# Transposing DMA transfers in place of TensorE turns, from the fifth group on, in a gated linear attention with a maxout feed-forward

## The chip, the cores and the metric

The kernel runs on one core of a Trainium2 chip. The metric is the device time of one execution in microseconds; smaller is better. The engines are TensorE (PE, with its weight loads PEld), VectorE (DVE), ScalarE (ACT), GpSimd (POOL) and SyncE (SP). SyncE computes nothing here: it issues the DMA transfers of the inputs and of the output. GpSimd issues those of the four weight matrices.

## The reference, cut to what matters

Four batches, eight heads, 768 steps, 48 channels a head. Each head carries a 48 x 48 state that decays channel by channel; the output of all heads is a row of 384 for each token, and the rows go through a maxout feed-forward.

```python
for t in range(S):                      # q, k, v, alpha: (4, 8, 768, 48), float32
    state = alpha[:, :, t, :, None] * state + np.einsum('bhd,bhe->bhde', k[:, :, t], v[:, :, t])
    y[:, :, t] = np.einsum('bhd,bhde->bhe', q[:, :, t], state)
...
h = np.maximum(np.maximum(x @ w1, x @ w2), x @ w3)     # x: (3072, 384), w: (384, 768)
return (h @ w_out).astype(np.float32)                  # w_out: (768, 384)
```

## The kernel before, in words

**Tiles.** A group `n` (0 to 11) is 256 tokens of one batch, all heads; `c, b = divmod(n, 4)`. A unit `u` is half the heads of a group, `u = 2n` or `2n + 1` (0 to 23). A partition of the input tiles holds two neighbouring tokens (`r` = 0, 1) of a block of 128 tokens; 64 partitions are one block (`i` = 0, 1).

**Steps of a group.** `load` (L262, SyncE) brings alpha, q, k and v, 384 KB each, into five buffers each. `decay` (L317) takes logarithms of alpha and group totals (`hp`). `prep(u)` (L380) makes running sums of the logarithms on TensorE (`Lp`, L389), exponentials of both signs (`ep`, `en`, L398), weights q and k with them (`qk`, L403, on GpSimd or VectorE), and turns them so that channels lie on partitions: `tp` (L421) is 16 TensorE transposes of 64 x 128 into two PSUM banks, and `qkT` (L429) one VectorE copy of 128 x 1024 out of them. Scores `A` (L441) are 16 small products of the turned k and q, and `LA` (L449) masks them. `state(n)` (L456) sums the new state (`pp`, L472) and carries it on (`Z`, L373). `output(n)` (L496) adds the part of the old state (`yi`, L509) and of the scores (`ya`, L531); for each of the two blocks, `xb` (L543) scales the result into 128 x 384, `xp` (L551) turns it with three TensorE products by a permutation matrix `order`, which also puts the tokens back in their order, and `xT` (L556) copies it out of PSUM.

**Feed-forward.** `ffn(n)` (L560) uses `w2 - w1` and `w3 - w1` (`wcat`; the differences `d`, L281): 36 products, `gp` (L575), in six steps of six per group: three column pairs `j`, each for gate `g` = 0 and 1. `h0` and `h1` (L584, L591) take the maxima. `op` (L603, L606) gives the output of one block, `ob` copies it, and `out` (L618, SyncE) stores it. `past` (L307) is `w1 @ w_out`.

**Order.** Every piece above is a step of a `Plan`, numbered as the loops create it (before: 0 to 810). A string, `ORDER`, lists all steps in the sequence in which they are issued: `24P3` is step 24 on TensorE with PSUM bank 3, and the letters P, V, A, G, S stand for TensorE, VectorE, ScalarE, GpSimd and SyncE. It was made ahead of time; nothing is chosen on the chip. Every engine works through its own tokens in this sequence and waits where an operand isn't ready. So on SyncE a transfer that waits holds all behind it. The four weight transfers (`weights`, L272) are tokens of GpSimd's sequence: w1, w2 and w3 are tokens 6, 7 and 10 of GpSimd's.

Of the kernel before, what the change touches and what calls it, by code (L numbers as in the profile page):

```python
# [23 lines left out]


ORDER = """
6S 0S 3S 1S 2S 52S 5S 7S 8V 9A 4S 10A 11G 17P0 54S 18V 13A 53S 19A 14P1 98S 28P2 12A 20A 55S 29V
15A 22V 100S 30A 31A 21V 99S 56V 101S 24P3 16G 143S 58A 32V 145S 57A 33V 74P5 144S 59P6 25V 62P7
35P0 146S 23A 63V 205S 26P2 64A 36V 272S 65A 34A 206S 75V 37P0 67G 27V 207S 60A 40P47 77A 274S 76A
61G 339S 66V 208S 42V 78G 69P2 38V 273S 39G 79V 41V 73G 81P5 68A 102G 82V 70V 83P0 80G 104A 44P4  # L30
85G 84V 86P56 45P2 87V 71P0 88V 46A 119P3 72V 103A 47P5 90P2 49A 120V 91P4 122A 193P0 92V 95A 105P1
121A 89V 108P4 93P2 48A 43V 96P3 50P6 123V 51A 94A 124V 109V 126P5 111A 97A 195P7 189V 106A 187V
196A 262P2 127V 321P3 194A 188V 128P5 110A 113V 254P1 112G 129V 258P7 255A 130G 329P0 115P4 192V
330A 197P1 107G 116V 114A 125G 331P6 198A 190V 117P4 325P0 322A 118V 147G 148A 256P1 191V 149A
131P34 263A 257V 153P5 259A 264P2 154V 133V 326A 132V 164P1 260P7 156A 265V 327P0 165V 261V 167A
135P3 323P2 166A 332V 155A 136P7 324V 169G 201P1 140V 158G 150P6 199P5 202A 137A 157V 151A 168V
160P2 328V 171P6 203P1 159A 170G 172V 200A 161V 173P6 204A 175P05 209G 174V 162P2 333P1 211A 163V
276G 277A 210A 218P6 269P7 334A 152G 219V 539S 278A 176V 275S 134V 221A 340S 177V 220A 141P2 229P3
138P1 341S 285P4 222G 230V 179P0 139A 266P6 142V 406S 231A 286V 342S 232A 223V 288A 234G 279P1
180P2 270A 267V 287A 212P3 178V 392P7 181A 233V 213A 296P6 225P4 280A 215G 184A 297V 236P2 290G  # L40
394P1 226V 299A 298A 237V 301G 182P0 393A 388P4 183V 344A 185P5 343G 238P2 395V 224A 227P6 336P0
186A 228V 289G 235A 389A 214G 239V 217G 390P1 337A 216G 345A 292P5 338S 300G 240P74 473S 293V 363P0
352P2 396P3 408S 353V 241V 474S 354A 463P5 391V 397A 268S 242G 398P6 335S 291A 282G 243V 409S 461P7
464A 281G 364V 302G 407S 399V 366A 459P3 284G 271S 365A 244V 476S 245P1 355A 246P5 460V 307P60 671S
357G 247P 462V 605S 294P2 251A 465P4 283G 295V 248A 356G 252P7 411A 455P5 253A 308V 368G 457P1 456A
466V 249P2 359P6 410G 458V 250A 303P3 346P5 529P2 304V 310G 412A 525P1 360V 309G 347A 530A 367G
305P3 311V 369A 361P5 521P7 306V 526A 349G 350G 358A 312P2 523P0 351G 522A 362V 543G 313P1 413P3
419P4 430P7 314P 414A 431V 370P5 420V 433A 467P3 524V 315A 435G 371V 318A 421A 477G 372P0 422A
374P25 545A 470P6 436G 479A 375V 478A 348G 373V 376G 432A 379P4 434G 480P2 471A 403P7 468A 424V
377V 486P0 319P1 423G 404A 531P6 487V 378V 488A 405S 380P3 527P7 481A 532V 608S 320A 541S 489A 381P  # L50
609G 528V 544A 475S 426P1 437P5 382A 540S 415G 316P0 427V 503G 400P7 317A 438V 416G 385V 383P4
552P1 401V 386P2 384A 591P0 483V 387A 402S 553V 484G 428P5 672S 592A 439P3 675G 497P7 555A 655P2
440V 554A 425G 593P0 611A 485G 498V 589P1 500A 418V 429V 491G 546P3 499A 653P4 587P7 417G 654A 594V
441P56 547A 676A 490V 563P4 533P3 442V 588V 443G 444G 656V 661P0 534A 501G 564V 447P5 535S 663P7
590V 662A 606S 492G 677A 446P2 445V 657P3 674S 565A 502G 664V 542S 566A 493P0 448P 658V 472S 482G
556G 504P6 607S 494V 508P4 624A 469S 659P3 452A 449V 610A 618P0 505V 595P1 450P5 453P2 596V 597P6
451A 454A 509V 536P7 660V 511G 549G 619V 568G 598V 621A 506P1 495P4 620A 678P3 551G 537A 725P6 496V
569G 679A 538S 684P0 612P7 719P3 557G 673S 685V 507V 665P4 567G 550V 686A 629P5 695P1 548V 599P2
510V 613A 720A 681V 623V 666A 615V 683V 723P7 622G 696V 630V 698A 602P3 724V 631A 614G 558G 687A
726V 635A 688G 721P4 697A 600V 603A 512P7 700G 601S 513P0 722V 632A 625P1 667S 514P 604S 626V 699G  # L60
574P6 515A 559P3 570P1 518A 727P5 634G 571V 701A 519P7 575V 729P0 616G 728A 560V 577G 516P1 668P2
633G 517V 730V 520V 627P5 669A 572P3 689V 561P0 737P7 670S 617V 573V 731P2 738A 562V 741P7 732A
578P3 576V 745P4 742A 628V 690A 579P0 636P1 580P 637V 640P7 581A 691P5 584V 638P1 746A 582P3 692V
747P0 583A 641V 644P4 743P5 639V 642G 739P6 643G 680V 585P3 645P7 740V 702P1 586A 646P 682V 706P3
703V 647A 734P6 650A 748V 707V 744V 704P1 709G 693P3 759P7 708G 735V 694V 755P0 757P5 705V 711P6
752P3 710P4 761P1 753A 756A 754S 648P2 712P 760A 733S 651P3 649A 749P0 762V 652A 716V 713V 777P7
750A 763P2 751S 736S 717P1 714P3 781P6 718A 779P4 782V 765P0 715V 783P1 778V 799P6 764V 801P3 766V
800A 773P7 784V 775P2 758V 793P0 780V 797P6 774V 795P1 791P5 767P4 792V 802V 770P7 776V 768A 796V
769S 794V 785P5 798V 771V 803P3 786V 772S 787S 807P4 804P 808P 805V 788P2 809A 806S 810S 789A 790S
"""  # L70


# [41 lines left out]
def kernel(  # L114
# [12 lines left out]
    nc = tc.nc  # L127

    B, H, S, D = q.shape
# [3 lines left out]
    P = 128  # L133
    HALF = P // 2
# [6 lines left out]
    UB = 2  # L141
# [13 lines left out]
    both = np.eye(2)  # L155
# [30 lines left out]
    NL, NQ, NT_, HH = 5, 6, 4, H // 2  # L186
    ld = {x: homes(NL, [P, H, 2, D], FP32, x + "n") for x in "aqkv"}
# [49 lines left out]

    live = {}
    LEAD, SLOPE = 5.5, 1.9
    WAFTER = {2: (0,), 4: (1,), 7: (2,), 11: (3,)}  # L240

    def copy(eng, out, in_):
        (nc.scalar.copy if eng == "ACT" else nc.vector.tensor_copy)(out=out, in_=in_)  # L243
# [136 lines left out]
    def prep(u):  # L380
# [1 line left out]
        hs = slice(hh * HH, (hh + 1) * HH)  # L382
        la, ep, en = las[n % 3], eps[u % 3], ens[u % 3]
        qk, v16 = qks[u % NQ], v16s[u % NQ]
        Lk, tk, Ak = ("Lp", u), ("tp", u), ("A", u)

        def cums(eng):
# [11 lines left out]
                          out=t, in_=live[Lk], func=AFT.Exp, scale=sign),  # L399
                      reads=[Lk, (Lk, 0)], writes=[(x, u % 3)])  # L400
        for w, x, e in ((0, "q", ep), (1, "k", en)):
            plan.step("qk", "POOL DVE", u,
                      lambda eng, w=w, x=x, e=e: on[eng].tensor_mul(  # L403
                          qk[:, w, :, :, :D].rearrange("p r h d -> p h r d"),
                          ld[x][n % NL][:, hs], e),
                      reads=[(x, n % NL, hh), ("ep" if w == 0 else "en", u % 3)],
                      writes=[("qk", u % NQ, w)])
        plan.step("v", "POOL ACT", u,
# [4 lines left out]
        def trans(eng):  # L413
            live[tk] = banks2(tk, FP16)[:, :, :4 * P]
            for w in range(2):
                for j in range(2):
                    for r in range(2):
# [4 lines left out]
                                                qk[rows, w, r, 2 * j:2 * j + 2, :],  # L422
                                                ident[rows, rows])

        plan.step("tp", "PE", u, trans, banks=[tk],
                  reads=[("qk", u % NQ, 0), ("qk", u % NQ, 1)],
                  writes=[tk])
        plan.step("qkT", "DVE", u,
                  lambda eng: nc.vector.tensor_copy(  # L429
                      out=qkT.rearrange("p i w j t -> p i (w j t)"), in_=live[tk]),  # L430
                  reads=[tk], writes=[("qkT", u % NT_)])

        def scores(eng):
            live[Ak] = banks2(Ak, FP32)
# [21 lines left out]
    def state(n):  # L456
# [6 lines left out]
        def sums(eng):  # L463
            for k in keys:
                live[k] = bank(k, [P, NP, 2 * D], FP32)
            for hh in range(2):
                qk, v16 = qks[us[hh] % NQ], v16s[us[hh] % NQ]
                for j in range(2):
                    for r in range(2):
                        for i in range(n_i):  # L470
                            rows = slice(i * HALF, (i + 1) * HALF)
                            nc.tensor.matmul(live[keys[i]][:, 2 * hh + j, :],  # L472
                                             qk[rows, 1, r, 2 * j:2 * j + 2, :],
                                             v16[rows, 2 * j:2 * j + 2, r, :],
                                             start=(r == 0), stop=(r == 1))

# [19 lines left out]
    def output(n):  # L496
# [43 lines left out]
        for i in range(UB):  # L540
# [4 lines left out]
                          eng, xb, live[yk].rearrange("p a b -> p (a b)"), ysc),  # L545
                      reads=[yk], writes=[("xb", m % 3)])

            def turn(eng, xb=xb, xk=xk):
                live[xk] = bank(xk, [P, NFT, P], FP32)
                for ft in range(NFT):  # L550
                    nc.tensor.matmul(live[xk][:, ft, :], xb[:, ft * P:(ft + 1) * P], order,  # L551
                                     start=True, stop=True)

            plan.step("xp", "PE", rank, turn, banks=[xk], reads=[("xb", m % 3)], writes=[xk])
            to = xTs[n][:, :, i * P:(i + 1) * P]
            plan.step("xT", "DVE ACT", rank, lambda eng, to=to, xk=xk: copy(eng, to, live[xk]),  # L556
                      reads=[xk], writes=[("xT", n, i)])


    def ffn(n):  # L560
# [32 lines left out]
        for i in range(UB):  # L593
# [4 lines left out]
            for lo, hi in parts:  # L598
                def shrink(eng, i=i, ok=ok, lo=lo, hi=hi):
# [5 lines left out]
                    for kt in range(lo, hi):  # L605
# [8 lines left out]
                          + ([("xT", n, i)] + [("past", kt) for kt in range(NFT)]) * (lo == 0))  # L614
            plan.step("ob", "ACT DVE", r, lambda eng, m=m, ok=ok: copy(eng, obs[m % 4], live[ok]),
                      reads=[ok], writes=[("ob", m % 4)])
            plan.step("out", "SP", -2.0,
                      lambda eng, i=i, m=m: nc.sync.dma_start(  # L618
                          out[b * S + (2 * c + i) * P:b * S + (2 * c + i + 1) * P, :], obs[m % 4]),
                      reads=[("ob", m % 4)])  # L620

    load(0, 0, HH, "aqk")
# [52 lines left out]
```

## Time and profile before

| | us |
|---|---|
| median of 2 timed runs (151.75 to 153.57) | 152.66 |
| the profiled execution | 153.0 |
| its span, first to last instruction | 151.2 |
| TensorE busy | 133.5 |
| VectorE busy | 120.7 |
| ScalarE busy | 82.3 |
| GpSimd busy | 69.3 |

How to read the profile: it is one execution, times in microseconds from the start of the span. "xN" is a number of instructions. The 40 slices give the busy share of each fortieth of the span in tenths. A group names the line, engine, operation and tiles, then busy time and mean duration. "SPq" is SyncE issuing a transfer; the time from there to the landing of the data is listed apart. A line with three numbers and slashes gives the shortest, the median and the longest duration in ns. TensorE's products overlap, so the sum of their durations is longer than the time that they take. The granted TensorE clock is 0.998 of full speed.

### The profile page before, as it was taken

How to read it: one execution, taken by the hardware profiler on the slowest of the kernel's cores; microseconds unless marked ns; L12 is line 12 of the kernel's file. 1: busy time of each engine (PE TensorE's matmuls, PEld its weight loads, DVE VectorE, ACT ScalarE, POOL GpSimd, SP SyncE). 2: the span in 40 equal slices, each digit the busy share in tenths (PEclk: the TensorE clock that was granted, in tenths of full speed). 3: DMA queues.
4: the chain of work that ended last, by engine and by line, in shares of the span. 5: the costliest groups of instructions: out<-in, count | busy, mean ns of one | idle time of the engine just before them, and what ended most of it. 6: DMA issues, size and time to landing. Idle time of an engine off the chain costs nothing.

```text
span 151.2 us, 5265 instructions
## 1 busy us (share of the span) xinstructions
PE 133.5 (88%) x2220; PEld 102.4 (68%) x2220; DVE 120.7 (80%) x210; ACT 82.3 (54%) x185; POOL 69.3 (46%) x106
## 2 busy tenths in 40 slices
PE   0145498999999999999999999998999999999991
PEld 0133276677766778888677878766868877888660
DVE  3188988769999999999698998899899992395920
ACT  3467246829576996777967756536627305210111
POOL 8114920080390697798992865688800220000000
PEclk9999999999999999999999999999999999999999
DMA  5999999999999999999529929960410002300124
GB/s 127 273 261 261 266 213 211 240 249 221 279 260 262 262 252 261 282 310 270 114 59 259 290 60 259 255 191 0 160 56 0 4 4 81 127 4 0 52 104 156
DMA packets 55880, 26.45 MB, mean 175 GB/s; under 512 B 50737, under 2 KB 55857, under 8 KB 55857
## 3 DMA queue, kind: packets, MB, share of 16 engines
q1 hardware_dynamic: 53440, 23.60, 63.5%
q0 software_dynamic: 1984, 2.36, 9.0%
q8 instruction: 17, 0.28, 0.8%
q10 hardware_dynamic: 432, 0.17, 0.5%
q14 instruction: 7, 0.05, 0.1%
HBM read 23.76 MB, written 4.72 MB: 188 GB/s over the span
## 4 chain that ended last, share of the span: by engine, by line
PE 74%; DMA 11%; SPq 5%; DVE 3%; issue 3%; ACT 2%; POOL 1%; ACTq 0%; DVEq 0%; POOLq 0%
PE psum L575 31%; PE psum L606 14%; PE psum L603 7%; DMA wcat<-in_moe_w_dram 7%; SPq L262 5%; PE psum L441 4%; DMA qn<-in_q_dram 4%; PE psum L421 4%; PE psum L531 3%; PE psum L472 3%; PE psum L551 2%; PE psum L307 2%; PE psum L509 2%; PE psum L389 1%; DVE Z L373 1%
## 5 line engine op out<-in xcount | busy, mean ns | idle before, releaser
L575 PE MATMUL psum<-xT,wcat 128*128 128x256 f16 x432 | 55.3, 277 | 0.3 <-DVE wcat L281 0.3
L575 PEld LDWEIGHTS <-wcat 128*128 128x128 f16 x432 | 40.7, 99 | 6.6 <-DVE wcat L281 0.5
L449 DVE TENSOR_TENSOR LA<-psum,d 128x1024 f16<-128x1024 f32 x24 | 28.8, 1219 | 3.8 <-PE psum L441 2.6
L606 PE MATMUL psum<-wo,hT 128*128 128x384 f16 x144 | 27.3, 326 | 0.0
L591 DVE TENSOR_TENSOR hT<-psum,hT 128x512 f16<-128x512 f32 x36 | 23.8, 681 | 3.2 <-PE psum L531 2.8
L403 POOL TENSOR_TENSOR qk<-qn,ep 128x384 f16<-128x384 f32 x16 | 16.7, 1052 | 14.5 <-ACT ep L398 14.0
L243 ACT COPY ob<-psum 128x384 f32<-128x384 f32 x17 | 8.1, 484 | 24.7 <-PE psum L606 24.7
L403 POOL TENSOR_TENSOR qk<-kn,en 128x384 f16<-128x384 f32 x15 | 15.0, 1001 | 13.0 <-ACT en L398 8.5
L606 PEld LDWEIGHTS <-hT 128*128 128x128 f16 x144 | 14.1, 98 | 9.3
L584 ACT ACTIVATE hT<-psum 128x512 f16<-128x512 f32 x25 | 14.6, 600 | 8.1 <-PE psum L575 7.9
L429 DVE COPY qkT<-psum 128x1024 f16<-128x1024 f16 x24 | 16.0, 684 | 1.4 <-PE psum L421 1.1
L603 PE MATMUL psum<-past,xT 128*128 128x384 f16 x72 | 15.7, 327 | 0.0
L421 PE MATMUL psum<-d,qk 64*128 64x64 f16 x384 | 10.6, 200 | 5.2 <-DVE qk L403 4.0
L398 ACT ACTIVATE en<-psum 128x384 f32<-128x384 f32 x24 | 11.8, 496 | 5.3 <-DVE psum L393 4.1
L398 ACT ACTIVATE ep<-psum 128x384 f32<-128x384 f32 x24 | 11.7, 492 | 4.6 <-POOL qk L403 2.9
L373 POOL TENSOR_TENSOR Z<-U,G 48x192 f16<-48x192 f32 x12 | 6.0, 504 | 16.3 <-DVE U L486 15.8
L421 PEld LDWEIGHTS <-qk 64*128 64x128 f16 x384 | 8.1, 100 | 8.0 <-DVE qk L403 5.3
L243 ACT CAST xT<-psum 128x384 f16<-128x384 f32 x19 | 8.8, 483 | 6.0 <-PE psum L551 5.7
L324 POOL TENSOR_TENSOR aa<-an 128x384 f32<-128x384 f32 (+1 forms) x11 | 10.7, 972 | 2.6 <-DMA an<-in_alpha_dram 2.5
L247 ACT ACTIVATE xb<-psum,c 128x384 f16<-128x384 f32 x17 | 9.4, 580 | 4.2 <-PE psum L531 4.1
L586 DVE TENSOR_SCALAR hT<-psum 128x512 f16<-128x512 f32 x11 | 7.5, 686 | 4.4 <-PE psum L575 4.3
L247 ACT ACTIVATE v<-vn,c 128x384 f16<-128x384 f32 x14 | 8.6, 617 | 4.3 <-DMA vn<-in_v_dram 3.9
(54 smaller groups left out, 193.8 us busy)
## 6 DMA issues: line engine op xcount, KB each, us to landing
out_dram<-ob SPq DMA_DIRECT2D x24, 192.0 KB, 2.0
an<-in_alpha_dram SPq DMA_DIRECT2D x11, 384.0 KB, 6.1
kn<-in_k_dram SPq DMA_DIRECT2D x11, 384.0 KB, 5.9
qn<-in_q_dram SPq DMA_DIRECT2D x11, 384.0 KB, 6.5
vn<-in_v_dram SPq DMA_DIRECT2D x11, 384.0 KB, 6.1
wcat<-in_moe_w_dram POOLq DMA_DIRECT2D x2, 576.0 KB, 11.3
w1s<-in_moe_w_dram POOLq DMA_DIRECT2D x1, 576.0 KB, 8.0
wo<-in_moe_w_out_dram POOLq DMA_DIRECT2D x1, 576.0 KB, 7.6
```

What stands on the lines that cost most here:

```text
L243: (nc.scalar.copy if eng == "ACT" else nc.vector.tensor_copy)(out=out, in_=in_)
L247: nc.scalar.activation(out=out, in_=in_, func=AFT.Copy, scale=factor)
L398: lambda eng, t=t, sign=sign: nc.scalar.activation(out=t, in_=live[Lk], func=AFT.Exp, scale=sign),
L403: lambda eng, w=w, x=x, e=e: on[eng].tensor_mul(qk[:, w, :, :, :D].rearrange("p r h d -> p h r d"), ld[x][n % NL][:, hs], e),
L421: nc.tensor.transpose(live[tk][:, i, at:at + HALF], qk[rows, w, r, 2 * j:2 * j + 2, :], ident[rows, rows])
L429: lambda eng: nc.vector.tensor_copy(out=qkT.rearrange("p i w j t -> p i (w j t)"), in_=live[tk]),
L449: lambda eng: nc.vector.tensor_mul(LA.rearrange("p a j r t -> p (a j) (r t)"), live[Ak].rearrange("p a (j t) -> p (a j) t", j=2), maskA.un ...
L575: nc.tensor.matmul(live[gk][:, jj, :], wcat[:, kt, g, c0:c0 + P], xT[:, kt, :], start=(kt == 0), stop=(kt == NFT - 1))
L584: nc.scalar.activation(out=h, in_=live[gk], func=AFT.Relu)
L591: lambda eng, h=h, gk=gk: nc.vector.tensor_max(h, live[gk], h),
L603: nc.tensor.matmul(live[ok], xT[:, kt, i * P:(i + 1) * P], past[:, kt, :], start=(kt == 0), stop=False)
L606: nc.tensor.matmul(live[ok], hT[:, kt, i * P:(i + 1) * P], wo16[:, kt, :], start=False, stop=(kt == NJ - 1))
```

## The change

Two constants, `DQ = DX = 4`, mark the first group that is treated in the new way.

- For units of groups 4 to 11 (16 units), `tp` and `qkT` are gone. A step `dq` on SyncE issues two transposing DMA transfers instead, one per block, each from 64 partitions x 1024 columns of `qk` straight into `qkT`.
- For these units the columns of `qk` are laid out so that a head pair's two tokens lie side by side, and each weighting is done by two instructions, one per pair of heads (`qk2`); the sums `pp` read the same columns in the new place.
- For the 16 blocks of these groups, `xp` and `xT` are gone. A step `dx` on SyncE issues one transposing transfer from `xb` (128 x 384) into `xT`. The tokens stay in the turned order, even ones first, and the store of the output is issued as two transfers of 64 rows each, every second row of the output.
- `ORDER` is new from the first token on, for 779 steps. SyncE now has 52 loads, 16 `dq`, 16 `dx` and 24 `out` tokens. GpSimd's w1, w2, w3 are tokens 7, 10 and 17 of its own sequence; ahead of w3 stand, among others, weightings of units 4, 5 and 6.

```diff
+    DQ, DX = 4, 4
...
+        qkx = qk.rearrange("p w r h d -> p (w r h d)").rearrange(
+            "p (w j r a d) -> p w j r a d", w=2, j=2, r=2, a=2)
+        cross = n >= DQ
...
+            def weigh(eng, w=w, x=x, e=e):
+                src = ld[x][n % NL][:, hs]
+                if not cross:
+                    on[eng].tensor_mul(qk[:, w, :, :, :D].rearrange("p r h d -> p h r d"), src, e)
+                else:
+                    for j in range(2):
+                        part = slice(2 * j, 2 * j + 2)
+                        on[eng].tensor_mul(
+                            qkx[:, w, j, :, :, :D].rearrange("p r a d -> p a r d"),
+                            src[:, part], e[:, part])
...
+            def swap(eng):
+                for i in range(UB):
+                    rows = slice(i * HALF, (i + 1) * HALF)
+                    nc.sync.dma_start_transpose(
+                        qkT[:, i].rearrange("p w j (r s) -> p (w j r) s", r=2),
+                        qk[rows].rearrange("p w r h d -> p (w r h d)"))
+
+            plan.step("dq", "SP", u, swap, reads=both, writes=[("qkT", u % NT_)])
...
+                            if n >= DQ:
+                                key = qk[rows, 1].rearrange("p r h d -> p (r h d)")[
+                                    :, (2 * j + r) * P:(2 * j + r + 1) * P]
...
+            else:
+                plan.step("dx", "SP", rank,
+                          lambda eng, to=to, xb=xb: nc.sync.dma_start_transpose(to, xb),
+                          reads=[("xb", m % 3)], writes=[("xT", n, i)])
...
+            rows = out[b * S + (2 * c + i) * P:b * S + (2 * c + i + 1) * P, :]
+            if n >= DX:
+                rows = rows.rearrange("(s r) d -> r s d", r=2)
+
+            def store(eng, rows=rows, m=m):
+                if len(rows.shape) == 2:
+                    nc.sync.dma_start(rows, obs[m % 4])
+                else:
+                    for r in range(2):
+                        nc.sync.dma_start(rows[r], obs[m % 4][r * HALF:(r + 1) * HALF, :])
```

## The prediction

> **What bounds the kernel now.** I read the page's busy line and its slices first, then the chain, then TensorE's instructions in order of time, then the SyncE queue and the landing times of its transfers.
>
> ```profile
> span 151.2 us, 5265 instructions
> PE 133.5 (88%) x2220; PEld 102.4 (68%) x2220; DVE 120.7 (80%) x210; ACT 82.3 (54%) x185; POOL 69.3 (46%) x106
> ...
> PE   0145498999999999999999999998999999999991
> ...
> DMA  5999999999999999999529929960410002300124
> ```
>
> From about 28 us to 148 us TensorE has no empty slice, and the DMA engines are full up to about 75 us, then free in places. The waits of TensorE in 28 to 148 us come to 0.8 us. So the kernel is a start, a closed stream of products, and a tail of 3.3 us. The chain in order of time shows what ends the start: the second weight matrix.
>
> ```profile
> 16.76 10.67 DMA wcat<-in_moe_w_dram
> 27.53 0.57 DVE wcat L281
> 28.14 2.74 PE psum L575 x12
> ```
>
> What one step is worth to the stream is the distance to the next start, not its duration:
>
> ```profile
> 52.25 0.25 PE L389 MATMUL psum<-la,c 128*128 128x192 f16 x1
> 52.43 0.64 PE L421 MATMUL psum<-d,qk 64*128 64x64 f16 x32
> 53.00 0.83 PE L575 MATMUL psum<-xT,wcat 128*128 128x256 f16 x6
> 53.67 0.33 PE L551 MATMUL psum<-d,xb 128*128 128x128 f16 x3
> 53.83 0.82 PE L575 MATMUL psum<-xT,wcat 128*128 128x256 f16 x6
> ```
>
> Two tp steps (32 transposes) take 0.57 us, so one takes 0.29; an xp step takes 0.16 to 0.18 (0.18 used); a gp step 0.66. In the same way A is 0.30, ya 0.52, yi 0.20, pp 0.45, Lp 0.20, hp 0.12, an op 1.46. Adding these along the order of before, from the first gp on, gives 119.1 us; the profile has 28.1 to 147.9, 119.8. The units are good to 0.7 us.
>
> The SyncE queue and its landings:
>
> ```profile
> L262 SPq DMA_DIRECT2D kn<-in_k_dram x13: 418/1067/8338, 0.7 to 97.8; - x13
> L262 SPq DMA_DIRECT2D an<-in_alpha_dram x13: 496/1294/3515, 1.2 to 68.8; - x13
> L262 SPq DMA_DIRECT2D qn<-in_q_dram x13: 385/1416/3292, 2.3 to 89.8; - x13
> L262 SPq DMA_DIRECT2D vn<-in_v_dram x13: 380/783/2107, 6.0 to 91.0; - x13
> ```
>
> ```profile
> L618 SPq DMA_DIRECT2D out_dram<-ob x24: 332/359/3108, 57.5 to 148.4; - x24
> ```
>
> A load holds SyncE for 0.4 us when the queue is free and for 1.4 when it is full; a store for 0.36 us. A store lands 4.1 us after its issue (median) while loads run (66 to 100 us) and 1.9 us after it later. This queue has slack now; it is where the change puts everything.
>
> **The change, part by part.** I numbered the steps of both orders as the loops make them, and put every SyncE token of the new order against the TensorE work listed ahead of it ("stream time": first gp at 28.1).
>
> *Removed, TensorE.* 16 tp at 0.29 and 16 xp at 0.18: 7.5 us. The new order also has 1.9 us more work ahead of the first gp (10.05 against 8.17 us). From the first gp on 109.7 us are left: 28.1 + 109.7 + 0.7 + 3.3 gives a span of 141.8 us if nothing waits. This is the gain to be had: 9.4 us.
>
> *Removed, VectorE and ScalarE.* 16 qkT copies at 684 ns (10.9 us of VectorE) and 16 xT copies at 483 to 551 ns. TensorE hardly waits for either in the stream (1.1 us for qkT by its weight loads, inside the 7.5), so no further gain: 0.
>
> *Split products.* Each weighting becomes two of 192 columns. On GpSimd two cost 2 x 504 ns (the row of Z at 192) against 1,000, on VectorE 2 x 357 (aa at 192) against 550: 9 of them, 1.5 us, under the 10.9 us that VectorE is freed of. 0; without that cover at most 1.5.
>
> *Second store from group 4 on.* 16 more issues of 0.36 us; one is at the end: +0.4 on the span.
>
> *A start listed anew.* GpSimd starts the weights. Before, the second and third follow the first at 16.8 and 19.1 us. In the new order the third (gate 1) stands behind qk of group 3, which reads q of group 3, the load that before was issued from 27.7 to 31.0 us behind three weights. With two weights ahead of it, each worth (31.0 - 15.8)/3 = 5.1 us of the queue, its issue ends near 25.9; 6.6 us to landing, 1.0 for the product: the third weight starts near 33.5, lands 7.6 to 8.0 us later, and after 0.6 us of differences the first gate-1 product can start at 42.1 us. Stream time has it at 28.1 + (16.58 - 10.05) = 34.6, the listed work up to it. I take +7.5 us. Bounds: 0 if loads and weights share otherwise; +11.2 if it lands in 11.3 us like wcat before.
>
> *Added: 48 transposing DMAs on SyncE* (32 of 64 x 1024, 16 of 128 x 384). No row shows one. Low end: a store, 0.36 us of SyncE, landing 1.6 us after its issue ends. High end: the load in a full queue, 1.44 us. I take 1.14, the mean of the loads' four medians, since a transpose is cut into small pieces as the loads are (384 bytes there) and not as the stores (1,536). For the landing I take the store amid loads, 4.1 us from the start, 2.96 after the issue, and 0.76 after it once the loads are over; a load is taken at 0.45, a store at 0.36.
>
> What is queued behind them: SyncE waits in order, so a dq whose qk isn't ready holds loads and stores too, and a load lost there delays the next qk. The cover is the TensorE work listed between the transfer and its reader: 4.0 to 8.2 us for dq, 1.8 to 7.9 for dx. Two examples. The dq of unit 12 has dq 11, dq 10, a load and both dx of group 4 in front, free to start at 52.7: 52.7 + 4 x 1.14 + 0.45 + 2 x 1.14 + 2 x 1.14 = 62.2, lands 65.2, and A of unit 12 stands at 61.8: 3.4 late (1.2 of it already due to dq 11). The second dx of group 8 stands only 1.8 us ahead of its product and needs 1.14 + 2.96: 2.3 late. Down the whole queue in this way: dq 11 1.2, dq 12 2.2, dx 5 0.9, dq 15 0.9, dx 6 0.5, dx 8 2.3, dq 20 0.4, dx 9 1.6, dx 10 and a small one 0.5: 10.5 us of new waits. At the low end it is 0.2, with 1.44, loads at 1.40 and stores at 0.80 it is 24 to 37.
>
> [...] The rows bound a transposing DMA only by its neighbours. [...]
>
> *Sum.* 141.8 + 7.5 + 10.5 + 0.4 = 160.2 us of span. The profiled execution took 153.0 us at a span of 151.2 (+1.8); the median of the timed runs, 152.66, is 0.3 under it. So 160.2 + 1.8 - 0.3 = 161.7, rounded to 162.
>
> **Rivals.**
> - *The transfers are hidden* (on the other side: not slower). Place: dq and dx on SyncE. At the store's price the leads hold and 0.2 us of waits remain: 141.8 + 7.5 + 0.2 + 0.4 + 1.5 = 151.4. It decides where the waits stay under 4.5 us (155.7 or less): issues under 0.6 us at the landings taken, or under 1.05 us if they land 1.6 us after the issue. For it: leads of mostly 4 us and more, free DMA slices after 75 us. Against: stores amid loads land in 4.1 us.
> - *The weights come in time as well*: no 7.5, 143.9. For it: the order of before met its weights to 0.8 us. Against: the load of q 3 above.
> - *Weights in time, queue as forecast*: 154.2.
> - *SyncE and the DMA rings become the bound.* The transposes add 5.8 MB to 26.5 MB, queue behind loads, and every issue costs a full queue's price: 24 to 37 us of waits, 175 to 188. For it: loads held SyncE 1.4 us each up to 56 us. Against: slices of DMA at 0 to 4 tenths after 105 us. [...]
>
> **How the numbers follow.** Forecast 0.48, its own range 155 to 169 (issues 0.95 to 1.3 us, weights +4 to +11). Hidden 0.15, hidden with weights in time 0.12, weights in time alone 0.07, rings the bound 0.18. Two per cent of 152.66, about what a measurement of this kernel can tell from no change, puts the limits at 149.6 and 155.7: faster 0.12; within, 0.15 + 0.07 = 0.22; slower, 0.48 + 0.18 = 0.66. The range 148 to 181 leaves out the fastest case (0.12) and the upper part of the slowest (0.08), 0.2 together.
>
> **What would show it.** In the profile after: DMA_TRANSPOSE issues on SyncE with a mean of 1 us or more, landing 3 us or more later; TensorE idle before the scores (A) and before gate products, released by DMA, some 8 to 12 us; the first gate-1 product later than 38 us; VectorE busy near 110 us. The prediction is wrong if these waits are under 2 us, if the issue takes under 0.5 us or over 2 us, or if the gate-1 weights land before 36 us.

## The result, and the profile after

The changed kernel takes 184.96 us (median of 2 runs, 183.75 to 186.17) against 152.66: slower, ratio 1.2116, 95% interval 1.1656 to 1.2576. The forecast of 162 had the direction and not the size. The profiled execution took 186.17 us, its span is 184.4.

First the page of the changed kernel: busy line, slices, and the shares of the chain.

```profile
span 184.4 us, 4767 instructions
PE 140.7 (76%) x1916; PEld 100.7 (55%) x1916; DVE 123.3 (67%) x223; ACT 72.8 (39%) x162; POOL 65.4 (35%) x116
PE   0245549967999989299798699978769869499960
PEclk9999999999999999969999699999987987969996
DMA  6999999999949978499996999699868965516154
...
PE 36%; SPq 23%; DMA 18%; DVE 14%; ACT 3%; issue 3%; POOL 1%; DVEq 0%; POOLq 0%
```

Before, TensorE had no empty slice from 28 us on; now it has holes all along. It runs 304 instructions fewer and is busy 7.2 us longer: PEclk, before at 9 in every slice, drops to 6 to 8 in several. In the chain SyncE's issues (SPq) went from 5% to 23%.

SyncE's instructions by line (three numbers: shortest, median and longest, in ns), with the landings counted from the start of the issue:

```profile
L447 SPq DMA_TRANSPOSE qkT<-qk x32: 1200/1262/2533, 51.5 to 153.2; - x32
DMA to landing us min/median/max: 2.6/3.3/5.6
...
L587 SPq DMA_TRANSPOSE xT<-xb x16: 1179/1206/3180, 70.5 to 164.5; - x16
...
L657 SPq DMA_DIRECT2D out_dram<-ob x32: 466/593/2153, 129.8 to 181.2; - x32
```

A transposing issue never takes less than 1.18 us here. The mean is 1.41, since some are held longer, up to 3.18; what held those is not shown. From 51.4 to 165.8 us, 114.4 us, SyncE is held for 101.1: 44.8 by the 32 transfers of q and k, 22.8 by the 16 of the outputs, 17.0 by 24 loads (0.71 each), 16.4 by 22 stores (0.75). (The texts of the experiments say 1.45, 0.77 and 103.5: they count the short gaps between neighbouring issues as held.) That queue is nearly full, and works in order: in the rows of it below, no issue starts before the one ahead of it has ended.

What TensorE waits for, in order of time, and SyncE at one of these places:

```profile
77.16 0.24 PE L461 MATMUL psum<-qkT 48*64 48x128 f16 x2 [2.40 <-DMA qkT<-qk]
91.20 2.12 PE L606 MATMUL psum<-xT,wcat 128*128 128x256 f16 x18 [1.17 <-DMA xT<-xb]
102.91 1.46 PE L606 MATMUL psum<-xT,wcat 128*128 128x256 f16 x6 [1.78 <-DMA xT<-xb]
160.61 1.20 PE L606 MATMUL psum<-xT,wcat 128*128 128x256 f16 x6 [2.35 <-DMA xT<-xb]
```

```profile
95.23 1.81 SPq L447 DMA_TRANSPOSE qkT<-qk  x1
97.14 1.21 SPq L587 DMA_TRANSPOSE xT<-xb  x1
98.39 0.57 SPq L262 DMA_DIRECT2D kn<-in_k_dram  x1
99.02 1.25 SPq L587 DMA_TRANSPOSE xT<-xb  x1
100.31 0.58 SPq L262 DMA_DIRECT2D qn<-in_q_dram  x1
```

The xT issued at 99.02 comes behind two transposes and a load without a gap, and its reader starts at 102.91, 3.9 us later. The loads behind it are late in turn. By the waits of the whole kernel, GpSimd stands 14.9 us for alpha (2.5 before), 13.1 for k (4.6 before) and 12.7 for v.

### The profile page after: what moved, and what is told of

The parts are those of the page before. It is cut to its first block, busy times and chain, and to the rows that moved or that the text cites. A ratio compares the mean times of both kernels' runs of the same rounds, so it can differ in the third digit from the quotient of the medians.

```text
span 184.4 us, 4767 instructions
## 1 busy us (share of the span) xinstructions
PE 140.7 (76%) x1916; PEld 100.7 (55%) x1916; DVE 123.3 (67%) x223; ACT 72.8 (39%) x162; POOL 65.4 (35%) x116
## 2 busy tenths in 40 slices
DMA packets 80197, 32.19 MB, mean 175 GB/s; under 512 B 75056, under 2 KB 80176, under 8 KB 80176
## 4 chain that ended last, share of the span: by engine, by line
PE 36%; SPq 23%; DMA 18%; DVE 14%; ACT 3%; issue 3%; POOL 1%; DVEq 0%; POOLq 0%
PE psum L606 18%; SPq L262 11%; DMA xT<-xb 6%; SPq L447 6%; PE psum L637 6%; DMA qn<-in_q_dram 4%; DMA out_dram<-ob 3%; SPq L587 3%; DMA vn<-in_v_dram 3%; DVE LA L469 3%; PE psum L634 3%; DVE qk L408 2%; SPq L657 2%; DVE qk L412 2%; PE psum L496 2%
## 5 line engine op out<-in xcount | busy, mean ns | idle before, releaser
L606 PE MATMUL psum<-xT,wcat 128*128 128x256 f16 x432 | 59.3, 289 | 9.4 <-DMA xT<-xb 6.1
L412 POOL TENSOR_TENSOR qk<-kn,en 128x192 f16<-128x192 f32 x24 | 13.8, 600 | 14.5 <-DMA kn<-in_k_dram 13.1
L412 POOL TENSOR_TENSOR qk<-qn,ep 128x192 f16<-128x192 f32 x22 | 12.8, 603 | 15.1 <-ACT ep L401 10.0
L634 PE MATMUL psum<-past,xT 128*128 128x384 f16 x72 | 16.4, 337 | 0.4 <-DVE U L510 0.4
L461 PE MATMUL psum<-qkT 48*64 48x128 f16 x384 | 11.4, 240 | 4.3 <-DMA qkT<-qk 3.7
L401 ACT ACTIVATE en<-psum 128x384 f32<-128x384 f32 x24 | 11.2, 488 | 8.0 <-DVE psum L396 6.6
L324 POOL TENSOR_TENSOR aa<-an 128x384 f32<-128x384 f32 (+1 forms) x7 | 6.6, 942 | 20.2 <-DMA an<-in_alpha_dram 14.9
L432 PE MATMUL psum<-d,qk 64*128 64x64 f16 x128 | 5.4, 225 | 10.0 <-DVE qk L408 8.8
L392 PE MATMUL psum<-la,c 128*128 128x192 f16 x24 | 6.2, 282 | 8.7 <-ACT la L334 7.9
L461 PEld LDWEIGHTS <-qkT 48*64 48x64 f16 x384 | 7.4, 116 | 8.7 <-DMA qkT<-qk 4.3
L617 DVE TENSOR_SCALAR hT<-psum 128x512 f16<-128x512 f32 x14 | 9.5, 684 | 1.7 <-PE psum L606 1.7
L432 PEld LDWEIGHTS <-qk 64*128 64x128 f16 x128 | 3.7, 114 | 12.2 <-DVE qk L408 9.6
```

Of the source, the lines that this page charges most:

```text
L401: lambda eng, t=t, sign=sign: nc.scalar.activation(out=t, in_=live[Lk], func=AFT.Exp, scale=sign),
L412: on[eng].tensor_mul(qkx[:, w, j, :, :, :D].rearrange("p r a d -> p a r d"), src[:, part], e[:, part])
L461: nc.tensor.matmul(live[Ak][i * HALF:(i + 1) * HALF, p, at:at + P], qkT[rows, i, 1, j, r * HALF:(r + 1) * HALF], qkT[rows, i, 0, j, :], st ...
L606: nc.tensor.matmul(live[gk][:, jj, :], wcat[:, kt, g, c0:c0 + P], xT[:, kt, :], start=(kt == 0), stop=(kt == NFT - 1))
L634: nc.tensor.matmul(live[ok], xT[:, kt, i * P:(i + 1) * P], past[:, kt, :], start=(kt == 0), stop=False)
```

## Experiments

All but 16 and 17 are single runs, and differences under 2 us between them are not read; the kernel before took 152.9 to 153.9 us beside them. "Q" is the theory that SyncE's in-order queue is overfull; the others are named in the texts.

**1. The new order with the turns on TensorE.** Each tp with its copy stands where dq stood, each xp where dx stood.

```diff
-    DQ, DX = 4, 4
+    DQ, DX = 12, 12
```

> The changed kernel with its new order, but every turn back on TensorE: each dq is a tp and a qkT copy at the same place of the order (or at the next place where two PSUM banks are free), each dx an xp and an xT copy on ScalarE, stores undivided. Theory Q (SyncE's queue: a transposing DMA holds SyncE about 1.45 us, in order, so 48 of them and the loads and stores behind them set the pace): the queue falls free, the late start of about 11 us and 7.5 us of turns on TensorE stay: 155 to 165 us. Theory O (the new order itself is what loses the time): 175 us or more. Theory R (the DMA engines and the landing of data are what is short): as Q, 155 to 165, since the transposes' bytes are gone too.

189.3 us. Useless as a test: TensorE, itself in order, now meets each tp directly ahead of the copy out of PSUM and waits for it (11.0 us of its waits end with a copy `qkT`, 4.3 with an `xT`). Run 11 mends that.

**2. Plain copies of the same bytes**, without transposing, at the same places.

```diff
-                    nc.sync.dma_start_transpose(
-                        qkT[:, i].rearrange("p w j (r s) -> p (w j r) s", r=2),
-                        qk[rows].rearrange("p w r h d -> p (w r h d)"))
+                    nc.sync.dma_start(
+                        qkT[:, i].rearrange("p w j t -> p (w j t)"),
+                        qk[:, i].rearrange("p r h d -> p (r h d)"))
```

> The changed kernel with each transposing transfer replaced by a plain SBUF-to-SBUF copy of the same number of bytes into the same tile (the turn itself is left out, so the output isn't the reference's). Same order, same waits, same count of issues. Theory Q: an issue costs about 0.6 us instead of 1.45, 48 x 0.85 = 41 us of SyncE's 103.5 us are gone, and what remains is the late start and short landings: 153 to 162 us. Theory R: bytes and queue places are the same, so 175 to 185. Theory O: 175 or more.

165.85 us. The issue of the copy, by line:

```profile
L446 SPq DMA_DIRECT2D qkT<-qk x32: 465/551/1776, 51.2 to 135.2; - x32
```

0.55 us (median) in place of 1.26. 32.20 MB moved against 32.19, landing 3.0 us after the start against 3.3 (qkT) and 3.6 (xT). So the bytes aren't the price: the transposing is. The time lies between the ranges of Q and R, and run 3 shows why it is above Q's. The copies also make fewer packets (67,142 against 80,197), so this run does not tell SyncE's hold from work inside the DMA engines.

**3. The transfers left out**, the rest as in the change. The two transfers of `dq` go in the same way, and `ffn` reads a tile of an earlier group, `xTs[n % 4]`.

```diff
-                          lambda eng, to=to, xb=xb: nc.sync.dma_start_transpose(to, xb),
+                          lambda eng: None,
```

> The changed kernel with the 48 transposing transfers left out altogether: scores and feed-forward of groups 4 to 11 read what groups 0 to 3 left in the tiles. It shows the floor of the new order with its late start. Theory Q and theory R: 150 to 156 us (141.8 us of listed work and tail, and about 11 us of late start). Theory O: 165 or more.

166.34 us (span 164.6): as with plain copies. Those were wholly hidden. But I had expected 150 to 156: without any transfer and without any turn in groups 4 to 11, the new order still ends 12 us behind the kernel before (153.89 beside it). Runs 4, 9, 10 and 13 to 15 look for these.

**4. The weights early**: w2 and w3 (73G, 85G) directly behind w1 (39G).

```diff
-109V 150P3 39G 82V 122A 148A 41V ... 110A 73G 46A
+109V 150P3 39G 73G 85G 82V 122A 148A 41V ... 110A 46A
```

> The changed kernel with one edit of its order: the transfers of w2 and w3 stand right behind that of w1 on GpSimd, as in the kernel before, instead of 3 and 10 tokens later. Theory Q: the products start some 5 to 10 us earlier, but SyncE's stretch from the first dq to the last dx (114 us, 103.5 of them held) stays as long and only begins somewhat earlier: 176 to 183 us. If the late start alone is the cause: 170 us or less.

183.68 us. The third weight now starts at 20.4 us, 13.1 earlier, and the first gate-1 product at 45.90, as in the change (45.85). So the weights did not set the start.

**5. The order of before, with dq and dx in the places of tp and xT.**

```diff
-213A 296P6 225P4 280A 215G 184A
+213A 291P6 225S 276A 215G 184A
```

> The kernel before's own order, with the tp and qkT of groups 4 to 11 replaced by dq at the place of tp, and xp and xT by dx at the place of xT; the code is the changed kernel's. The start is that of before, the covers of the transfers are short. Theory Q: the same 48 holds of 1.45 us on SyncE, with less cover: 175 to 195 us, and the first product starts at 28 to 30 us. Theory O (the new order loses the time): 165 or less.

227.38 us, worse than any theory gave. TensorE's longest waits:

```profile
63.44 0.31 PE L462 MATMUL psum<-qkT 48*64 48x128 f16 x2 [9.45 <-DMA qkT<-qk]
88.39 2.74 PE L607 MATMUL psum<-xT,wcat 128*128 128x256 f16 x12 [11.62 <-DMA xT<-xb]
```

The order of before has a turn close ahead of its reader, where a transfer needs 3 to 4 us (3.3 and 3.6 to landing in the change). And SyncE stands for 40.9 us in front of stores whose `ob` isn't copied yet (18.1, 11.9 and 10.9 by its waits), with the transfers behind them. So the transfers can't be had at the places of the old turns.

**6. The stores on ScalarE's queue.**

```diff
-                    nc.sync.dma_start(rows, obs[m % 4])
+                    nc.scalar.dma_start(rows, obs[m % 4])
```

> The changed kernel with all stores of the output issued from ScalarE's queue instead of SyncE's; transposes and loads stay on SyncE. Theory Q: 22 issues, 16.9 us, leave SyncE's stretch between the first dq and the last dx: 165 to 176 us. Theory R (DMA engines short of time): the bytes are the same, so 181 to 186.

177.46 us, a span of 175.7 against 184.4 and 182.0 of the two runs of the change. All bytes and transposes remain, and taking 0.75 us a store off SyncE gives back 6 to 9 us. That is Q's direction, but the time lies between the two ranges.

**7 and 12. Only q and k by transfer**, the outputs on TensorE (in 12 xp and xT stand farther apart), and **8. only the outputs**.

```diff
-    DQ, DX = 4, 4
+    DQ, DX = 4, 12        # 7, 12
+    DQ, DX = 12, 4        # 8
```

> The changed kernel with dq kept (32 transposing transfers) and dx undone: xp on TensorE and xT on ScalarE at the place of dx, stores undivided. Theory Q: SyncE loses 16 x 1.45 + some 8 divided stores x 0.6, about 28 of 103.5 us: 165 to 175 us. Theory R: a quarter of the transposes' bytes gone, 178 to 184.

> The run with dq only once more, with xp and xT spread as in the run before this one. Theory Q: SyncE has slack already, so only the waits of TensorE for the xT copies go: 160 to 167 us. If dx leaving the queue is not what gave the 17 us: 175 or more.

> The changed kernel with dx kept (16 transposing transfers, divided stores) and dq undone: tp on TensorE and qkT on VectorE at the place of dq. Theory Q: SyncE loses 32 x 1.45 = 46 of 103.5 us and is no longer full; the late start stays: 158 to 168 us. Theory R: three quarters of the transposes' bytes gone, 160 to 168 as well.

167.77 and 169.55 us; 191.04. Two thirds of the transposes (32 of 48) cost about 2 us in the new order, 167.77 against 165.85 of plain copies: xp back on TensorE (2.9 us by the forecast's units) and the stores in one piece (2.9 by the table further down) about cancel. An issue is still 1.26 us there. The price comes with the last third. That fits a queue near full: SyncE is held 73 of the 90 us from the first transpose to the last in run 7, and 101 of 114 in the change. It would also follow if the outputs' transfers, with leads down to 1.8 us by the forecast, were the costly ones. No run keeps all 48 and lengthens those leads, and run 8, which has the outputs' transfers alone, has run 1's fault.

**9 and 10. The order of before for the first 249 (10: 248) tokens, then the new order**, with both kinds of transfers (9) or with dq alone (10).

```diff
-0S 3S 52S 2S 1S 98S 5S 8G 6S ...
+6S 0S 3S 1S 2S 52S 5S 7S 8V ...
```

> The changed kernel, with the first 249 tokens of its order taken from the order of the kernel before (up to the start of group 4's turns), the rest in the new order with PSUM banks given anew. Theory S (the listing of the start costs about 11 us on its own and adds to the queue): first gate-1 product near 33 us instead of 46, total 172 to 177. Theory Q alone (SyncE's full queue sets the end, wherever the products start): 180 to 186.

> As the run with the start of before, but only dq is moved to DMA: xp and xT stay on TensorE and the copy engines a few tokens after their xb, stores undivided. Theory S with theory Q: 16 transposes and 16 stores fewer free SyncE, and the start is that of before: 152 to 160 us. Theory Q alone, without S: 164 to 170, as the run with dq only.

184.33 and 169.27 us: no gain from an early start (in run 10 the first product of `gp` starts at 28.5 us; in the change it starts at 35.2, and the stream behind it at 40.0). Run 10 shows where the gain goes:

```profile
56.73 0.25 PE L346 MATMUL psum<-c,la 128*128 128x4 f16 x4 [3.16 <-ACT la L336]
64.19 0.42 PE L463 MATMUL psum<-qkT 48*64 48x128 f16 x16 [1.40 <-DVE LA L471]
67.19 0.64 PE L535 MATMUL psum<-Z,qkT 128*128 128x96 f16 x8 [2.40 <-DVE Z L375]
```

The stream catches up with what the new order lists late (logarithms of alpha, masks, states) and waits there.

**11. As run 1, each tp and xp spaced from its copy as before.**

```diff
-203P2 324V 225P3 226V 343G 344A
+243G 397A 225P2 455P0 391V 283G
```

> The first run once more, new order and all turns on TensorE, but with each tp some 14 tokens ahead of its scores and each copy some 4 to 6 tokens behind its product, as in the order of before, so that no engine waits at a turn's own copy. If the 189 us of the first run came from copies listed directly behind their products: 166 to 174 us, the 166 of the run without transposes and 7.5 us of TensorE work. If the new order itself can't carry the turns: 180 or more.

180.34 us. Slower than with plain copies by 14 us, so the new order doesn't carry the turns on TensorE either; where they lose the time was not followed up.

**13. The order of before, all turns of groups 4 to 11 left out. 14. The kernel before with split products alone. 15. Run 3 with unsplit products.**

```diff
-                if not cross:
+                if True:          # 15
...
+                for part in ([slice(0, 2), slice(2, 4)] if n >= 4 else [slice(0, 4)]):   # 14
+                    on[eng].tensor_mul(qk[:, w, :, part, :D]..., src[:, part], e[:, part])
```

> The order of before with every turn of groups 4 to 11 left out (no transfer, no TensorE turn, no copy; those groups read tiles that earlier groups left, so part of the computation is missing), the products split as in the change. Theory N (the new order itself costs the 23 us that the run without transfers showed in it): here nothing of that is left, the turns' 7.5 us go and the time is 145 to 148 us. Theory D (the split products slow VectorE and GpSimd beyond their cover): 153 us or more.

> The kernel before with one thing changed: from group 4 on each weighting of q and k is two products, one per pair of heads. All turns stay on TensorE. Theory N and the forecast's term: 0, so 152 to 154 us. Theory D: 156 us or more.

> The new order with every turn of groups 4 to 11 left out (the run that took 166.3 us; part of the computation is missing), and the weightings in one product each again. Theory N: 164 to 167 us, no change. Theory D: 160 us or less.

152.34, 154.74 and 163.03 us. Run 13 is the surprise: 16 tp and 16 xp gone, nothing in their place, and the kernel is hardly faster. TensorE from its first product of `gp` to its last product, before and in run 13 (columns: stretch, its length, then busy time of PE, PEld, DVE, ACT, POOL, the clock, the DMA share, GB/s):

```profile
28.14:147.83 119.69, 119.16 (x1930) 91.47 (x1930) 101.61 (x169) 67.29 (x151) 58.60 (x84) 1.00 0.66 163
```

```profile
28.16:145.44 117.28, 114.30 (x1626) 85.34 (x1626) 91.50 (x156) 61.55 (x138) 62.76 (x110) 1.00 0.71 165
```

It is busy 4.9 us less and idle 3.0 us in place of 0.5. The time lies between the two ranges, nearer to D's. The longest of the new waits:

```profile
102.10 0.81 PE L604 MATMUL psum<-xT,wcat 128*128 128x256 f16 x6 [1.40 <-ACT e L352]
```

Run 14: with the split the stream ends 1.7 us later in the order of before, which is not clear of the noise of single runs (154.74 us, and 153.87 for the kernel before beside it). Run 15 against run 3: 161.2 against 164.6 us of span, so the split costs 3.4 us in the new order; the time again lies between the two ranges.

**16 and 17. Candidates: the order of before, transfers in the last two groups only**, where loads are over, each directly behind what it reads (17: dq alone).

```diff
-    DQ, DX = 4, 4
+    DQ, DX = 10, 10       # 16
+    DQ, DX = 10, 12       # 17
```

> The order of before, with the new turns only in the last two groups (DQ = DX = 10), where all loads are issued and SyncE has little left to do; each transfer stands right behind what makes it ready (q and k weighted, xb), 4 to 11 TensorE steps ahead of its reader. The 4 tp and 4 xp are worth 1.9 us at most. If the price of the change is SyncE full of loads and transposes, nothing is held up here: ratio 0.985 to 1.00. If a transposing transfer is too slow in itself (1.2 us of issue, 2.3 at least to landing, two in a row ahead of the last group's products, which stand 6 steps away), 1.00 to 1.02.

> As the run with both in the last two groups, but only q and k are turned by transfers there; the outputs stay on TensorE. 4 tp, 1.2 us at most. SyncE full as the cause: ratio 0.99 to 1.00. Slow in itself: 1.00 to 1.01.

Run 17: 154.81 us against 152.87, ratio 1.0126, interval 1.0081 to 1.0171. That is less than two per cent, but the interval leaves out 1, and it fits the second answer (slow in itself), a little over its upper end. The split weightings of four units are in it too. Run 16 took 152.99 to 157.51 us in six runs, too widely spread for a ratio. Run 17 in a queue without loads:

```profile
L449 SPq DMA_TRANSPOSE qkT<-qk x8: 1221/1247/2547, 106.1 to 120.1; - x8
DMA to landing us min/median/max: 2.6/3.0/4.4
```

Two issues of 1.25 us and a landing come to some 4.3 us for a unit, even alone; TensorE waits 2.4 us for qkT (three times, at most 1.2) to save 1.2. No run here that computes everything beats the kernel before.

**18. The outputs' transposes issued by ScalarE.**

```diff
-                          lambda eng, to=to, xb=xb: nc.sync.dma_start_transpose(to, xb),
+                          lambda eng, to=to, xb=xb: nc.scalar.dma_start_transpose(to, xb),
```

> The changed kernel with one word changed: the 16 transposing transfers of the outputs (dx) are issued by ScalarE, at the same places of the order, and those of q and k stay on SyncE. All 48 transfers and their bytes stay. Theory Q (SyncE, in order, is held 1.45 us by each and everything queued behind is late): 168 to 175 us, since SyncE is freed of 23 us of its 103 and ScalarE, busy 73 of 184, can carry them. Theory R (the DMA rings or the transposing itself are the limit, whoever issues): 182 us or more.

199.4 us, and it does not tell Q from R, because a new wait came with it:

```profile
SPq L447 <- DMA xT<-xb: 26.7, 7, 8.2
```

SyncE's transposes of q and k wait 26.7 us for ScalarE's transposes to land, seven times and at most 8.2 us, though they share no tile. In the change, with all transposes on SyncE, no wait of SyncE ends with a transpose's landing. So a second queue was no relief for the transposes here.

## Why the prediction was right or wrong, point by point

The profiled spans, cut at the end of TensorE's last product, give a bridge from before to after in single steps (us):

| kernel | last product ends | rest | span |
|---|---|---|---|
| before | 147.8 | 3.4 | 151.2 |
| 14: split products alone | 149.5 | 3.4 | 152.9 |
| 13: turns left out as well, and two stores | 145.4 | 5.2 | 150.6 |
| 3: and the new order | 158.3 | 6.3 | 164.6 |
| 2: and the 48 transfers as plain copies | 157.3 | 6.8 | 164.1 |
| after: and they transpose | 178.1 | 6.3 | 184.4 |

| step | forecast | measured |
|---|---|---|
| turns off TensorE | -7.5 | -4.1 |
| split products | 0 | +1.7 (not clear of noise) |
| new order (1.9 less work left behind the first gp, 7.5 late start) | +5.6 | +12.9 |
| bytes of the transfers | 0 | -1.0 |
| transposing | +10.5 | +20.8 |
| second store, at the end | +0.4 | +2.9 |
| sum | +9.0 | +33.2 |

Each is a difference of single runs, good to about 2 us. Three steps of the prediction failed: the listed TensorE work was taken for the time, the start was costed by the weights and by quiet rows of VectorE, and SyncE's queue was priced too low.

**The gain of 7.5 us** failed at the step "from the first gp on 109.7 us are left", which took the listed TensorE work for the time. The trace of before shows TensorE closed, but not what stands close behind it. VectorE was at 80%. In run 13 TensorE waits for the others instead, for ScalarE's `e` most (1.8 us in two places). Against run 14, which has the split too, its busy time falls by 6.2 us and its idle time grows by 2.3, so about 4.1 of the 7.5 are left; against the kernel before it is 2.4.

**The split products** were costed at nothing under VectorE's freed time. On GpSimd the halves take 600 ns each (median 588 to 592), not the 504 of the row used. On VectorE 12 of the 18 halves take 0.35 us as forecast; the other six run while GpSimd computes beside them, and take 0.64 to 1.83 us. The cover did not appear either: VectorE was to be busy near 110 us and is busy 123.3. The copies `qkT` are gone, but its weightings take 17.3 us in place of 10.5, and the new order gives it more of the other steps (six `aa` in place of two, 50 steps of `hT` in place of 47). The price of the split in the new order is 3.4 us.

**The start** was right in its first part and wrong in its cause. The third weight was issued at 33.50 us, as forecast, and landed 8.2 later. But the differences came late, as VectorE's rows show:

```profile
22.76 2.73 DVE L408 TENSOR_TENSOR qk<-qn,ep 128x384 f16<-128x384 f32 x1 [1.94 <-DMA qn<-in_q_dram]
...
37.70 1.78 DVE L408 TENSOR_TENSOR qk<-kn,en 128x384 f16<-128x384 f32 x1
39.41 1.01 DVE L281 TENSOR_TENSOR wcat<-wcat,w1s 128x768 f16<-128x768 f16 x2
...
45.25 0.55 DVE L281 TENSOR_TENSOR wcat<-wcat,w1s 128x768 f16<-128x768 f16 x1
```

VectorE, without a gap of more than 0.4 us from 25 to 47 us, reaches the difference for gate 1 at 45.25, and the first gate-1 product starts at 45.85: 11.2 us behind its listed work in place of 7.5. (The upper bound of +11.2 comes to 10.8 by its own terms, 33.5 + 11.3 + 0.6 - 34.6, and is about what came, by another cause.) The two weightings shown take 2.73 and 1.78 us, where 0.55 is usual in both kernels; GpSimd computes beside both. That the one draws out the other is not tested by a run that moves them apart. Run 4 excludes the weights, runs 9 and 10 exclude the start as a sum term: an early start is lost again to inputs that the new order brings late. Which of its tokens make the 12.9 us stays open; no run changed the places of the loads alone.

**The transposes on SyncE** were right in mechanism, and the term of 10.5 us was mis-sized. A transpose is cut into small pieces, as the 1.14 us took it: the change moves 24,064 packets more than run 3, which leaves the transposes out (80,197 against 56,133), all of under 512 B. But the price of each issue was too low: 1.14 against a mean of 1.41, loads 0.45 against 0.71, stores 0.36 against 0.75. By the forecast's prices the 48 transposes, 24 loads and 22 stores of the stretch hold SyncE for 73 us; measured, 101 of 114. Windows of TensorE from the stream's start to its last product, after and in run 2:

```profile
40.02:178.06 138.04, 120.40 (x1488) 85.30 (x1488) 94.49 (x168) 52.27 (x115) 44.40 (x83) 0.94 0.83 160
```

```profile
39.87:157.32 117.45, 112.53 (x1488) 81.74 (x1488) 95.21 (x168) 52.00 (x115) 45.05 (x83) 0.99 0.76 189
```

Idle: 138.04 - 120.40 = 17.6 against 4.9, so 12.7 us of new waits; the forecast had 10.5. TensorE names DMA for 9.8 of them, inside the 8 to 12 that the forecast wanted to see. That these come so near is luck. For the same 1,488 products TensorE is busy 120.4 us in place of 112.5, 7.9 more, because its clock falls to half five times (0.94 against 0.99 by the windows; last section), and such time is not simply added to the waits. Run 4, with the same 48 transposes, shows it:

```profile
38.97:174.91 135.94, 114.89 (x1488) 82.27 (x1488) 96.56 (x168) 52.12 (x114) 45.86 (x85) 0.99 0.84 163
```

Its clock falls once, it is busy 114.9 us, and it is idle for 21.0, 16.1 more than run 2. Its span, 181.9 us, is that of the second run of the change (182.0), and run 9, with the early start, has 182.6. So whether TensorE computes slowly or waits, the end hardly moves: transposing costs 17 to 21 us in this order, about twice the term, and the waits alone are not its measure. The landings, 3.3 to 3.6 us from the start, lie between the 4.1 taken amid loads and the 1.9 taken later.

**The second store** was costed as one issue of 0.36 us. A half store holds SyncE for 0.59, twelve stand at the end (from 173.5 us), and the last copy of `ob` waits for one to land, as the chain's end shows:

```profile
174.01 0.60 SPq L657
174.65 0.60 SPq L657
175.30 0.59 SPq L657
175.99 2.15 DMA out_dram<-ob
178.14 0.48 ACT ob L243
```

**The rivals.** "SyncE and the DMA rings become the bound" came, with 175 to 188 us, in its first half, as far as runs 6 and 7 show: SyncE's queue did. Its second half, that the bytes queue behind loads, is excluded by run 2. Whether the transposing itself slows the DMA engines stays open, since run 18 brought a wait of its own. "The transfers are hidden" holds for plain copies alone. Run 2 sets a transpose beside a plain copy of the same tile: the landing is nearly alike, 3.3 against 3.0 us, but the issue takes 1.26 against 0.55.

## What to carry to other kernels

Before taking work off the engine that is always busy, leave that work out once and time it: here 7.5 us of listed TensorE work were worth 2.4 to 4.1. Price a transfer by what it holds of its queue, and add up the queue: at the forecast's prices it was filled for 73 us, at the measured ones for 101 of 114, and the transposes cost about twice what was forecast. No run here shows a turn by transfer to pay; even in a queue without loads, two in a row need some 4.3 us ahead of their reader (run 17). And when a queue sets the end, time lost on another engine beside it can cost little (run 4 against the change).

## What the runs showed of the hardware

**In the changed kernel the TensorE clock fell to 0.50 for 3.41 us after 3.41 us in which TensorE was busy 1.70 us or less.** Windows of it (the number after POOL's is the clock), two falls with the stretch ahead of each, and then a stretch that no fall followed:

```profile
75.59:79.00 3.41, 0.84 (x19) 0.59 (x20) 0.14 (x1) 0.00 (x0) 0.00 (x0) 1.00 0.61 89
79.00:82.41 3.41, 3.41 (x56) 2.47 (x55) 2.07 (x3) 1.08 (x3) 0.96 (x1) 0.50 1.17 258
99.48:102.89 3.41, 1.64 (x46) 1.16 (x43) 1.34 (x3) 0.58 (x1) 0.00 (x0) 1.00 0.89 188
102.89:106.30 3.41, 3.40 (x17) 2.46 (x18) 3.02 (x8) 0.96 (x2) 2.80 (x6) 0.50 1.23 275
126.80:130.21 3.41, 2.22 (x27) 1.13 (x24) 3.41 (x8) 0.00 (x0) 3.10 (x6) 1.00 0.64 109
```

The five falls of the stream begin at 79.00, 102.89, 137.02, 150.68 and 160.92 us, whole multiples of 3.41 apart. TensorE is busy 0.84, 1.64, 1.70, 1.66 and 1.06 us in the 3.41 ahead of them. Each fall costs up to 1.7 us of TensorE's time, an estimate: half of 3.41. The idle time alone does not decide: in the change 1.71 to 2.57 us of it inside one stretch came ahead of each fall, while in run 4 TensorE is idle for 2.41 us across two neighbouring stretches, 1.09 and 1.32, and no fall follows:

```profile
154.21:157.62 3.41, 2.32 (x31) 1.50 (x31) 1.23 (x1) 0.00 (x0) 0.00 (x0) 1.00 0.54 114
157.62:161.03 3.41, 2.09 (x46) 1.71 (x47) 0.70 (x2) 0.97 (x2) 0.00 (x0) 1.00 0.29 59
161.03:164.44 3.41, 3.41 (x30) 2.62 (x28) 1.21 (x3) 1.19 (x2) 0.00 (x0) 1.00 0.29 58
```

In the change, the stream has 40 such stretches from 41.45 us on: a fall followed each of the five with at most 1.70 us of work, and none of the others, which have 2.22 or more. TensorE need not stand idle for a fall: 1.70 us of work, from 133.61 to 137.02 us, did not hold the clock.

**A transposing issue held SyncE for 1.2 us even where the loads were over** (1.22 shortest, 1.25 median in run 17), a plain copy of the same tile for 0.47 to 0.55 (shortest and median in run 2).

**Plain SBUF-to-SBUF copies of 5.8 MB disappeared beside the rest** (runs 2 and 3: 165.85 and 166.34 us).
